# Attention memory and gated FFN on one core: heads grouped even and odd, 32-wide column tiles on both row halves, one load queue

## The chip, the core and the metric

The kernel runs on one core of a Trainium2 chip. A core has a matrix engine (TensorE, PE in the profile, with its weight loads as PEld), a vector engine (DVE), a scalar engine (ACT), GpSimd (POOL) and a sync engine (SP) that here only issues DMAs. They run side by side and wait for each other on semaphores. Products go to PSUM, from where ACT or DVE must copy them to the main on-chip memory. The metric is the time of one execution on the device, in microseconds.

## The reference

Per batch (8) and head (8), softmax weights over 32 memory slots, made from `phi`, gather k and v over 576 tokens into a memory of 32 rows. Queries attend to that memory, and the heads together (512 wide) go through a gated feed-forward block.

```python
a = phi - np.max(phi, axis=2, keepdims=True)
a = np.exp(a)
a = a / (np.sum(a, axis=2, keepdims=True) + 1e-09)   # axis 2: the tokens
k_m = np.einsum('bhsm,bhsd->bhmd', a, k)
v_m = np.einsum('bhsm,bhsd->bhmd', a, v)
scores = scale * np.matmul(q, k_m.transpose(0, 1, 3, 2))
...
attn = attn / (np.sum(attn, axis=-1, keepdims=True) + 1e-09)
x = np.matmul(attn, v_m)                 # then [4608, 512] over all heads
g = x @ w_gate                           # 512 -> 1536
silu = g * (1.0 / (1.0 + np.exp(-g)))
val = x @ w_val
return (silu * val @ w_out)              # 1536 -> 512
```

All tensors are float32; d is 64 per head.

## The kernel before

The order of the work is written by hand: each engine takes its instructions in the order in which the code issues them. `x` is never formed. Since `x @ w = attn @ (v_m @ w)`, the kernel multiplies the 32 memory rows of each head with its 64 rows of the weights, `U = v_m @ w`, and then the attention weights with `U`. Four heads make a group of 128 rows (4 x 32), and two groups make the 8 heads.

For one batch the steps are, with their lines:

- **Loads.** `phi` and `q` come through SP's queue in float32 (L71, L85), k and v through GpSimd's queue, converted to bfloat16 on the way (L79, L80). GpSimd then casts q (L93). GpSimd also issues the loads of the weights, six blocks `W` (L101) and three blocks `WO` (L110).
- **Memory.** `phi_exp` (L122) is one ACT instruction. `kv_group` (L134) multiplies pairs of heads, 64 memory rows wide, with k and v of both heads (256 columns); only the diagonal halves are wanted. L144 sums the weights with a column of ones, L152 inverts, L155 scales and masks on DVE. `kv_T` transposes (L165, copy L167).
- **Queries.** `q_T` transposes two heads at a time (L173, copy L179).
- **Attention.** `scores` multiplies 128 x 64 blocks of the masked memory with the queries (L188), ACT takes the exp (L196). `z_norm` sums over each head's 32 rows with a block matrix of ones (L203); ACT takes Ln and exp(-x) (L205, L207), DVE multiplies (L209).
- **U.** `u_step` makes one tile of 128 x 512 from two products, 64 wide, contracted over 128 rows (L218). ACT (L227, seven of twelve) or DVE (L229, five of twelve) copies it. There are twelve steps a batch: 3 column blocks, gate and value, 2 groups.
- **Slots.** `gv_slot`: 24 a batch (12 blocks of 128 hidden columns, two halves of 288 tokens). Four products (L248) write gate and value into one buffer of two PSUM banks; ACT takes silu of the gate (L256), DVE multiplies with the value (L262) into `t_h`. The multiplication is issued one slot later.
- **Output.** Twelve products of 512 columns per tile of 128 tokens (L286), a copy by DVE (L298) or ACT (L296), and DMAs on SP (L300). A pair of batches has nine tiles; four follow the even batch, five the odd one.

PSUM is shared by three pools of two buffers each: `gv` (two banks a buffer), `s` (memory, transposes, U) and `o` (output).

The main loop, for batch b: `window(b)` loads ACT's table for exp and Ln, issues the scores, the exp of phi(b+1), and the normalisation, with up to 36 output products of batch b-1 between them. Then `interleave` issues the 24 slots of batch b and spreads the rest of the output products and the preparation of batch b+1 (memory, queries, U) over them by the weights in ns that stand ahead of each item. Batch 0 differs: its U steps stand between its slots, and batch 1's preparation follows them. The output tiles of the last batch come after everything.

Of the kernel before, what the change touches and what calls it, by code (L numbers as in the profile page):

```python
# [14 lines left out]
def kernel(  # L15
# [10 lines left out]
):  # L26

# [11 lines left out]
    NG = 2  # L39
# [21 lines left out]
    ident = consts.tile([128, 128], BF16, tag="ident", name="ident")  # L61
    mask = consts.tile([128, 128], FP32, tag="mask", name="mask")
    bones = consts.tile([128, 128], BF16, tag="bones", name="bones")
    ones1 = consts.tile([128, 1], BF16, tag="ones1", name="ones1")


    phis, kvs, qs, qf = {}, {}, {}, {}

    def load_phi(b):
        t = inp.tile([P, H, J, M], FP32, tag="phi", name="t_phi")  # L70
        nc.sync.dma_start(  # L71
            out=t.rearrange("p h j m -> p h (j m)"),
            in_=phi[b].rearrange("h (p j) m -> p h (j m)", p=P),
        )
        phis[b] = t
# [7 lines left out]
    def load_q(b):  # L83
        t = inp.tile([P, H, J, D], FP32, tag="qf", bufs=1, name="t_qf")
        nc.sync.dma_start(  # L85
            out=t.rearrange("p h j d -> p h (j d)"),
            in_=q[b].rearrange("h (p j) d -> p h (j d)", p=P),
        )
        qf[b] = t

    def cast_q(b):
        t = inp.tile([P, J, H, D], BF16, tag="q", bufs=1, name="t_q")
        nc.gpsimd.tensor_copy(out=t.rearrange("p j h d -> p h j d"), in_=qf.pop(b))  # L93
        qs[b] = t
# [23 lines left out]
    ephis, bkvs, kvTs, qTs, atts = {}, {}, {}, {}, {}  # L118

    def phi_exp(b):  # L120
        t = att.tile([P, J, H, M], BF16, tag="ephi", name="t_ephi")
        nc.scalar.activation(  # L122
            out=t.rearrange("p j h m -> p h j m"), in_=phis.pop(b), func=AF.Exp
        )
        ephis[b] = t

    def kv_group(b, g):

        pk = ps.tile([128, 2 * 2 * D + 1], FP32, tag="s", name="p_kv")
        te, tk = ephis[b], kvs[b]  # L130
        for j in range(J):
            for pp in range(2):
                pr = 2 * g + pp
                nc.tensor.matmul(  # L134
                    pk[64 * pp:64 * pp + 64, 0:4 * D],
                    lhsT=te[:, j, 2 * pr:2 * pr + 2],
                    rhs=tk[:, :, 2 * pr:2 * pr + 2, j * D:(j + 1) * D],
                    start=(j == 0),
                    stop=(j == J - 1),
                )  # L140
        for j in range(J):
            for pp in range(2):
                pr = 2 * g + pp
                nc.tensor.matmul(  # L144
                    pk[64 * pp:64 * pp + 64, 4 * D:4 * D + 1],
                    lhsT=te[:, j, 2 * pr:2 * pr + 2],
# [4 lines left out]
        r = att.tile([128, 1], FP32, tag="rS", name="t_rS")  # L151
        nc.vector.reciprocal(out=r, in_=pk[:, 4 * D:4 * D + 1])  # L152
        t = att.tile([128, 2, 128], BF16, tag=f"bkv{g}", name="t_bkv")
        for w in range(2):
            nc.vector.scalar_tensor_tensor(  # L155
                out=t[:, w], in0=pk[:, 128 * w:128 * w + 128], scalar=r, in1=mask,
                op0=ALU.mult, op1=ALU.mult,
            )
        bkvs[b, g] = t

    def kv_T(b):
        pT = ps.tile([128, 2, NG, 128], BF16, tag="s", name="p_T")
        for g in range(NG):
            for w in range(2):
                nc.tensor.transpose(pT[:, w, g], bkvs[b, g][:, w], ident)  # L165
# [74 lines left out]
    def gv_slot(b, s):  # L240
# [20 lines left out]
        def mul():  # L261
            nc.vector.tensor_tensor(out=dst, in0=sg, in1=p[:, 1, 0:HALF], op=ALU.mult)  # L262
# [182 lines left out]
```

## Time and profile before

| | us |
|---|---|
| median of 3 runs (lowest, highest) | 334.71 (334.39, 336.28) |
| the profiled execution | 334.37 |
| its span | 332.5 |
| TensorE / ACT / DVE / GpSimd busy in the span | 272.5 / 177.5 / 165.1 / 41.8 |
| slot products L248, 768, mean 288 ns | 126.4 |
| output products L286, mean 379 ns | 102.8 |
| U products L218, 192, mean 403 ns | 34.3 |
| memory products L134 and L144, 192 each | 14.8 and 5.6 |
| GpSimd's casts of q, 8, mean 2745 ns | 22.0 |
| ACT table loads, 17 of 1283 ns | 21.9 |

Busy time is the union of an engine's instructions. Products are pipelined, so their mean durations overlap: a product of 512 columns has a mean of 379 ns, though 24 of them pass in 5.18 us. Idle time of an engine that nothing waits for costs nothing. The chain of waits follows the work back from the last instruction, at each step to what released it.

### The profile page before, as it was taken

To read this page: it belongs to the slowest core of one execution; us is meant where nothing else is said; L and a number is where in the kernel's file an instruction comes from. 1 tells how busy PE (TensorE), PEld (TensorE's weight loads), DVE (VectorE), ACT (ScalarE), POOL (GpSimd) and SP (SyncE) were. 2 spreads that over 40 slices of the span, in tenths; PEclk is the share of its full clock that TensorE was granted. 3 is DMA by queue.
4 is the path that set the end of the run, shared out by engine and by line. 5 is a ranking of instruction groups with operands and counts; after the bars stand their busy time and mean duration, and the time that the engine had idled before them with its cause. 6 is when DMAs were issued, how large, how long until landed. Compare 5 with 4: busy or idle time off the path is not lost.

```text
span 332.5 us, 5356 instructions
## 1 busy us (share of the span) xinstructions
PE 272.5 (82%) x2076; PEld 159.3 (48%) x2096; DVE 165.1 (50%) x371; ACT 177.5 (53%) x333; POOL 41.8 (13%) x39
## 2 busy tenths in 40 slices
PE   0044587878989899989998999989898999898894
PEld 0033144534565456645664467446644575445541
DVE  1012345563567354855576446745673558455520
ACT  4000855438446855496448744794378455764501
POOL 8025030050013000500050001300030000000000
PEclk9999999999999999999999999999999999999998
DMA  7999999891588055943891284917201210030033
GB/s 177 231 206 205 251 230 261 148 140 36 139 182 131 2 129 140 185 63 78 208 182 16 60 209 111 137 35 174 64 0 29 69 42 24 2 95 0 2 95 95
DMA packets 35624, 38.08 MB, mean 115 GB/s; under 512 B 1808, under 2 KB 30992, under 8 KB 35600
## 3 DMA queue, kind: packets, MB, share of 16 engines
q1 hardware_dynamic: 18304, 23.60, 28.5%
q0 software_dynamic: 17296, 14.16, 27.9%
q8 instruction: 16, 0.26, 0.3%
q14 instruction: 8, 0.07, 0.1%
HBM read 42.47 MB, written 9.44 MB: 156 GB/s over the span
## 4 chain that ended last, share of the span: by engine, by line
PE 64%; DVE 15%; DMA 7%; ACT 7%; issue 3%; POOL 2%; another core or an unknown queue 1%; SPq 0%; ACTq 0%; POOLq 0%
PE p_oo L286 24%; PE p_gv L248 24%; DVE t_h L262 8%; PE p_u L218 8%; DMA W<-in_moe_w_gate_dram 6%; ACT t_sg L256 4%; PE p_kv L134 3%; DVE t_qT L179 2%; DVE t_U L229 2%; DVE t_bkv L155 2%; PE p_q L173 2%; PE p_sc L188 1%; PE p_z L203 1%; ACT t_U L227 1%; POOL t_q L93 1%
## 5 line engine op out<-in xcount | busy, mean ns | idle before, releaser
L248 PE MATMUL p_gv<-t_A,t_U 128*128 128x288 bf16 x768 | 126.4, 288 | 14.1 <-DVE t_h L262 13.0
L256 ACT ACTIVATE t_sg<-p_gv 128x288 bf16<-128x288 f32 x192 | 79.0, 411 | 93.9 <-PE p_gv L248 60.9
L262 DVE TENSOR_TENSOR t_h<-t_sg,p_gv 128x288 bf16<-128x288 bf16 x192 | 86.2, 451 | 44.7 <-ACT t_sg L256 44.5
L286 PE MATMUL p_oo<-WO,t_h 128*128 128x512 bf16 x412 | 102.8, 379 | 1.3 <-issue 1.0
L248 PEld LDWEIGHTS <-t_U 128*128 128x128 bf16 x768 | 70.5, 98 | 60.5 <-issue 31.2
L286 PEld LDWEIGHTS <-t_h 128*128 128x128 bf16 x432 | 41.7, 98 | 38.5 <-issue 1.6
L218 PE MATMUL p_u<-W,t_kvT 128*64 128x512 bf16 x192 | 34.3, 403 | 6.2 <-ACT t_U L227 4.2
L227 ACT CAST t_U<-p_u 128x512 bf16<-128x512 f32 x56 | 32.1, 586 | 9.9 <-PE p_u L218 8.8
L229 DVE CAST t_U<-p_u 128x512 bf16<-128x512 f32 x40 | 27.7, 691 | 18.0 <-PE p_u L218 16.8
L298 DVE COPY t_o<-p_oo 128x512 f32<-128x512 f32 x24 | 16.5, 689 | 35.7 <-PE p_oo L286 35.7
L134 PE MATMUL p_kv<-t_kv,t_ephi 96*64 96x256 bf16 x192 | 14.8, 294 | 18.6 <-DMA t_kv<-in_v_dram 18.6
L93 POOL CAST t_q<-t_qf 96x3072 bf16<-96x3072 f32 x8 | 22.0, 2745 | 52.5 <-PE p_q L173 30.4
L79 POOL DMA_DIRECT2D t_kv<-in_k_dram x8 | 6.3, 792 | 141.1 <-PE p_kv L144 102.3
L218 PEld LDWEIGHTS <-t_kvT 128*64 128x64 bf16 x192 | 11.1, 108 | 24.9 <-issue 23.1
L196 ACT ACTIVATE t_E<-p_sc 128x576 bf16<-128x576 f32 x16 | 9.6, 648 | 24.5 <-PE p_sc L188 24.5
L173 PE MATMUL p_q<-ident,t_q 96*128 96x96 bf16 x192 | 14.1, 214 | 8.6 <-POOL t_q L93 7.8
L209 DVE TENSOR_TENSOR t_A<-t_E,t_rz 128x576 bf16<-128x576 bf16 x16 | 12.1, 758 | 17.2 <-ACT t_rz L207 17.2
L134 PEld LDWEIGHTS <-t_ephi 96*64 96x64 bf16 x192 | 10.2, 117 | 21.7 <-issue 21.7
L179 DVE COPY t_qT<-p_q 128x576 bf16<-128x576 bf16 x32 | 14.5, 455 | 10.8 <-PE p_q L173 10.7
L152 DVE RECIPROCAL t_rS<-p_kv 128x1 f32<-128x1 f32 x16 | 2.7, 169 | 30.4 <-PE p_kv L144 30.4
L173 PEld LDWEIGHTS <-t_q 96*128 96x128 bf16 x192 | 11.9, 102 | 10.2 <-POOL t_q L93 7.9
L122 ACT ACTIVATE t_ephi<-t_phi 96x1536 bf16<-96x1536 f32 x8 | 11.8, 1477 | 4.2 <-DMA t_phi<-in_phi_dram 4.2
(31 smaller groups left out, 116.3 us busy)
## 6 DMA issues: line engine op xcount, KB each, us to landing
t_qf<-in_q_dram SPq DMA_DIRECT2D x8, 1152.0 KB, 7.8
t_phi<-in_phi_dram SPq DMA_DIRECT2D x8, 576.0 KB, 5.4
t_kv<-in_k_dram POOLq DMA_DIRECT2D x8, 576.0 KB, 8.3
t_kv<-in_v_dram POOLq DMA_DIRECT2D x8, 576.0 KB, 10.4
out_dram<-t_o SPq DMA_DIRECT2D x24, 192.0 KB, 2.3
out_dram<-t_o SPq DMA_DIRECT2D x24, 128.0 KB, 2.4
W<-in_moe_w_gate_dram POOLq DMA_DIRECT2D x3, 512.0 KB, 21.4
W<-in_moe_w_val_dram POOLq DMA_DIRECT2D x3, 512.0 KB, 23.1
```

The source lines that it names most:

```text
L93: nc.gpsimd.tensor_copy(out=t.rearrange("p j h d -> p h j d"), in_=qf.pop(b))
L134: nc.tensor.matmul(pk[64 * pp:64 * pp + 64, 0:4 * D], lhsT=te[:, j, 2 * pr:2 * pr + 2], rhs=tk[:, :, 2 * pr:2 * pr + 2, j * D:(j + 1) * D] ...
L173: nc.tensor.transpose(pq[:, P * j:P * (j + 1)], qs[b][:, j, 2 * pr:2 * pr + 2], ident[0:P, 0:P],)
L179: nc.vector.tensor_copy(out=t, in_=pq)
L218: nc.tensor.matmul(p[64 * pp:64 * pp + 64, :], lhsT=kvTs[b][:, 1, g, 64 * pp:64 * pp + 64], rhs=W[which, c][:, 2 * g + pp], start=True, st ...
L227: nc.scalar.copy(out=t, in_=p)
L229: nc.vector.tensor_copy(out=t, in_=p)
L248: nc.tensor.matmul(p[:, which, 0:HALF], lhsT=Us[b, which, c, g][:, 128 * r:128 * (r + 1)], rhs=atts[b, g][:, hf], start=(g == 0), stop=(g ...
L256: nc.scalar.activation(out=sg, in_=p[:, 0, 0:HALF], func=AF.Silu)
L262: nc.vector.tensor_tensor(out=dst, in0=sg, in1=p[:, 1, 0:HALF], op=ALU.mult)
L286: nc.tensor.matmul(box["p"], lhsT=hts[c, jf][:, 128 * u:128 * (u + 1)], rhs=WO[jf], start=(jf == 0), stop=(jf == NJF - 1),)
L298: nc.vector.tensor_copy(out=t_o, in_=box["p"])
```

## The change

The heads are grouped even and odd instead of by fours in order: group g holds heads g, g+2, g+4, g+6. In the contraction of U the two heads of a pair (2i, 2i+1) lie in the two halves of the 128 rows, 64 each; in that of the scores the halves hold two halves of the tokens. With that, three kinds of products are issued on part of the array, by an explicit place (row, column):

```diff
-    def kv_group(b, g):
-        pk = ps.tile([128, 2 * 2 * D + 1], FP32, tag="s", name="p_kv")
...
+    def kv_half(b, g):
...
         for j in range(J):
+            for i in range(NP):
                 nc.tensor.matmul(
+                    pk[32 * i:32 * i + 32, 2 * D * g:2 * D * (g + 1)],
+                    lhsT=ephis[b][:, j, g, i],
+                    rhs=kvs[b][:, :, 2 * i + g, j * D:(j + 1) * D],
...
+                    tile_position=(0, 32 * i),
+                )
```

The memory takes 48 products of 128 columns instead of 24 of 256, and no masked halves. The sums take 12 instead of 24. The mask goes; DVE normalises with one reciprocal and two multiplications (`bk`, `bv`) instead of two reciprocals and four masked products. k is written twice, so that after the transposes (3 instead of 4) it lies in both row halves; v of the even heads lies in rows 0 to 63 and that of the odd heads in rows 64 to 127.

```diff
     def scores(b, g):
+        p = gv_banks()
+        for i in range(NP):
+            for r in range(2):
                 nc.tensor.matmul(
+                    p[r][32 * i:32 * i + 32, 0:HALF],
+                    lhsT=kTs[b][64 * r:64 * r + 64, g, 32 * i:32 * i + 32],
+                    rhs=qTs[b, i][64 * r:64 * r + 64, g],
...
+                    tile_position=(64 * r, 32 * i),
...
+    def u_round(b, which, c):
+        p = [ps.tile([128, CH], FP32, tag="s", name=f"p_u{g}") for g in range(NG)]
+        for i in range(NP):
+            for g in range(NG):
                 nc.tensor.matmul(
+                    p[g][32 * i:32 * i + 32, :],
+                    lhsT=kTs[b][64 * g:64 * g + 64, 2, 32 * i:32 * i + 32],
+                    rhs=W[which, c][64 * g:64 * g + 64, i],
...
+                    tile_position=(64 * g, 32 * i),
+                )
+        for g in range(NG):
...
+            if g == 0:
+                nc.scalar.copy(out=t, in_=p[g])
+            else:
+                nc.vector.tensor_copy(out=t, in_=p[g])
```

A round replaces two U steps: eight products of 32 rows and 512 columns, contracted over 64, in place of four of 64 rows, contracted over 128. The token halves are now the two row halves of the queries (tokens whose place in a run of six is even or odd), so `token_segments` sends the output rows to other places.

The buffer of gate and value is split in two pools, `g` and `v`, of two buffers of one bank each. They serve scores and sums too, so exp and Ln are issued by halves of 288 columns.

```diff
+    def gv_banks():
+        return [
+            ps.tile([128, CH], FP32, tag=("g", "v")[r], name=f"p_{'gv'[r]}") for r in range(2)
+        ]
...
-        p = ps.tile([128, 2, 512], FP32, tag="gv", name="p_gv")
+        p = gv_banks()
```

Loads: q is converted by its DMA in GpSimd's queue, without a cast. The queue holds k, v and q of batch 0, the weights, and then phi, k, v and q of batch 1, 2 and so on. SP loads only the first phi.

```diff
     def load_q(b):
+        t = inp.tile([P, H, J * D], BF16, tag="q", name="t_q")
+        nc.gpsimd.dma_start(out=t, in_=q[b].rearrange("h (p j) d -> p h (j d)", p=P))
...
+    load_phi(0, nc.sync)
+    load_kv(0)
+    load_q(0)
...
+    load_phi(1, nc.gpsimd)
+    load_kv(1)
     load_q(1)
```

Order: batch 0's output products follow its slots at once; batch 1's window has none beside it; the first twelve slots of batch 1 have nothing between them, and batch 2's preparation follows in the other twelve. In the later windows four output products go ahead of the table load. Some output products are held back for the next batch.

```diff
+    run(out_list(0))
+    run(att_items(1))
+    run(u_items(1))
+
+    backlog = []
+    hold = {1: 0, 2: 12, 3: 12, 4: 14, 5: 14, 6: 16, 7: 0}
...
+        if b == 1:
+            interleave(slots[:12], [])
+            flush_mul()
+            exp_tables()
+            phi_exp(2)
+            interleave(slots[12:], att_items(2) + u_items(2))
```

What that does to three queues:

GpSimd at the start, before, from the fifth of the six weight blocks on:

```order
L101 DMA W_117<-in_moe_w_gate_dram 128x4x512
L101 DMA W_119<-in_moe_w_val_dram 128x4x512
L79 DMA t_kv<-in_k_dram 96x8x384
L80 DMA t_kv<-in_v_dram 96x8x384
L110 DMA WO_124<-in_moe_w_out_dram 128x4x512
L110 DMA WO_126<-in_moe_w_out_dram 128x4x512
L110 DMA WO_128<-in_moe_w_out_dram 128x4x512
L93 CAST t_q<-t_qf 96x8x6x64
```

GpSimd at the start, after the change, from its first load on:

```order
L72 DMA t_kv<-in_k_dram 96x8x384
L73 DMA t_kv<-in_v_dram 96x8x384
L78 DMA t_q<-in_q_dram 96x8x384
masks.py:197 MEMSET ident 128x128
masks.py:199 ISA
masks.py:199 AFFINE_SELECT ident<-ident 128x128
L86 DMA W_101<-in_moe_w_gate_dram 128x4x512
L86 DMA W_103<-in_moe_w_val_dram 128x4x512
```

q of batch 0 stood behind all weight loads and two loads of batch 1, as a cast; it is now the third load, ahead of the weights.

ACT in batch 1's window and slots, before (`t_E` exp of the scores, `t_ephi` of phi, `t_sg` silu of a slot):

```order
L348 ACT_TABLE_LOAD
L196 ACTIVATE t_E<-p_sc 128x576 x2
L122 ACTIVATE t_ephi<-t_phi 96x8x6x32
L205 ACTIVATE t_lz<-p_z 128x576
L207 ACTIVATE t_rz<-t_lz 128x576
L205 ACTIVATE t_lz<-p_z 128x576
L207 ACTIVATE t_rz<-t_lz 128x576
L256 ACT_TABLE_LOAD
L256 ACTIVATE t_sg<-p_gv 128x288 x8
L296 COPY t_o<-p_oo 128x512
L256 ACTIVATE t_sg<-p_gv 128x288 x9
```

ACT from the middle of batch 1's window on, after the change:

```order
L220 ACTIVATE t_lz<-p_v 128x288
L221 ACTIVATE t_lz<-t_lz 128x576
L273 ACT_TABLE_LOAD
L273 ACTIVATE t_sg<-p_g 128x288 x12
L365 ACT_TABLE_LOAD
L114 ACTIVATE t_ephi<-t_phi 96x4x6x32 x2
L273 ACT_TABLE_LOAD
L273 ACTIVATE t_sg<-p_g 128x288 x7
```

The exp of phi has moved out of the window into the middle of the slots, with a table load on either side.

DVE where a batch's U is made among the slots of the batch ahead of it, before:

```order
L229 CAST t_U<-p_u 128x512
L262 TENSOR_TENSOR t_h<-t_sg,p_gv 128x288
L229 CAST t_U<-p_u 128x512
L262 TENSOR_TENSOR t_h<-t_sg,p_gv 128x288 x2
L229 CAST t_U<-p_u 128x512
L262 TENSOR_TENSOR t_h<-t_sg,p_gv 128x288
```

DVE at a like place, after the change:

```order
L246 CAST t_U<-p_u_2263 128x512
L279 TENSOR_TENSOR t_h<-t_sg,p_v 128x288
L246 CAST t_U<-p_u_2286 128x512
L279 TENSOR_TENSOR t_h<-t_sg,p_v 128x288 x2
L246 CAST t_U<-p_u_2318 128x512
L279 TENSOR_TENSOR t_h<-t_sg,p_v 128x288
L246 CAST t_U<-p_u_2341 128x512
```

The pattern on DVE stays; each of its copies now belongs to a whole round (the other half of the round is ACT's), so a copy stands behind each round.

319 lines of the change are left out of this document (147 added, 172 removed).

## The prediction

> **What bounds the kernel now.** First the page's busy shares, and the shares of the chain that ended last:
>
> ```profile
> PE 272.5 (82%) x2076; PEld 159.3 (48%) x2096; DVE 165.1 (50%) x371; ACT 177.5 (53%) x333; POOL 41.8 (13%) x39
> PE 64%; DVE 15%; DMA 7%; ACT 7%; issue 3%; POOL 2%; another core or an unknown queue 1%; SPq 0%; ACTq 0%; POOLq 0%
> ```
>
> TensorE leads, but a third of the chain is something else. So I cut the span into five stages (view by stretches: the length, then busy time of PE, PEld, DVE, ACT, POOL, then the granted clock, DMA share and GB/s):
>
> ```profile
> 0.00:40.84 40.84, 10.83 (x97) 7.20 (x97) 6.78 (x25) 10.45 (x13) 14.90 (x22) 1.00 1.14 214
> 40.84:64.65 23.81, 18.91 (x114) 10.18 (x112) 12.67 (x27) 13.27 (x29) 2.74 (x1) 1.00 1.16 229
> 64.65:110.45 45.80, 40.56 (x359) 23.64 (x361) 26.79 (x61) 25.80 (x49) 8.55 (x6) 1.00 0.63 114
> 110.45:285.95 175.50, 164.65 (x1307) 97.99 (x1317) 101.34 (x226) 109.84 (x209) 15.57 (x10) 1.00 0.44 93
> 285.95:332.50 46.55, 37.52 (x211) 20.27 (x211) 17.50 (x34) 18.15 (x36) 0.00 (x0) 0.98 0.20 51
> ```
>
> A runs up to batch 0's first gate product, B over its 24 slots, C up to the window of batch 2, D over batches 2 to 6, E over batch 7 and the last output tiles. The granted clock is full (0.98 to 1.00), so only order and waits count. In A TensorE is busy 11 of 41 us; the chain in order of time and the timeline say why:
>
> ```profile
> 4.63 21.35 DMA W<-in_moe_w_gate_dram
> 26.26 0.74 POOL WO L110
> 27.00 2.76 POOL t_q L93
> 15.52 0.79 POOL L79 DMA_DIRECT2D t_kv<-in_k_dram  x1 [7.90 <-DMA t_kv<-in_k_dram]
> 18.63 1.49 PE L134 MATMUL p_kv<-t_kv,t_ephi 96*64 96x256 bf16 x12 [18.63 <-DMA t_kv<-in_v_dram]
> 29.81 1.14 PE L173 MATMUL p_q<-ident,t_q 96*128 96x96 bf16 x12 [7.82 <-POOL t_q L93]
> 40.84 3.88 PE L248 MATMUL p_gv<-t_A,t_U 128*128 128x288 bf16 x16
> ```
>
> k and v share the DMA engines with q and the second phi and land at 15.5 and 18.6. GpSimd's cast of q stands behind issues that wait for weights, so query transposes start at 29.8.
>
> In B, and in most of E, the slot loop is the bound:
>
> ```profile
> 52.55 0.90 ACT L256 ACTIVATE t_sg<-p_gv 128x288 bf16<-128x288 f32 x2 [0.74 <-PE p_gv L248]
> 52.99 0.94 DVE L262 TENSOR_TENSOR t_h<-t_sg,p_gv 128x288 bf16<-128x288 bf16 x2 [0.69 <-ACT t_sg L256]
> 53.50 1.14 PE L248 MATMUL p_gv<-t_A,t_U 128*128 128x288 bf16 x8 [0.50 <-DVE t_h L262]
> 55.13 0.66 PE p_gv L248 x4
> 190.40 0.49 PE p_gv L248 x4
> ```
>
> Two slots take 1.63 us (53.50 to 55.13), 0.82 each, while a slot's four products back to back take 0.49 (at 190.40). The product waits for DVE's multiplication, because one buffer holds both gate and value.
>
> **The change, stage by stage.**
>
> *A, the loads.* What the software queue does when it has the engines for itself:
>
> ```profile
> 66.65 0.77 POOL L79 DMA_DIRECT2D t_kv<-in_k_dram  x1 [21.59 <-PE p_kv L144]
> 67.41 0.77 POOL L80 DMA_DIRECT2D t_kv<-in_v_dram  x1
> t_kv<-in_k_dram POOLq DMA_DIRECT2D x1, 576.0 KB, 6.0
> t_kv<-in_v_dram POOLq DMA_DIRECT2D x1, 576.0 KB, 8.1
> 21.13 0.76 POOL L110 DMA_DIRECT2D WO<-in_moe_w_out_dram  x1 [1.58 <-DMA W<-in_moe_w_gate_dram]
> 23.67 0.74 POOL L110 DMA_DIRECT2D WO<-in_moe_w_out_dram  x1 [1.78 <-DMA W<-in_moe_w_val_dram]
> ```
>
> That k lands at 66.65 + 6.0 = 72.65 and v at 75.51: 2.86 us for 576 KB. Weight blocks land 2.54 apart (the two issues that wait for them). With bytes moving from about 3 us, phi, k, v and q are four times 2.86: v at some 11, q at some 14, and no cast behind it. From the cast's end (29.76) to the first gate product (40.84) took 11.1. Of that the exp of the next phi (1.48) leaves this window. Halved activations (four times 2 x 0.411 - 0.682 = 0.6, rows below) and the copies of the second round (0.1) come on top. First gate product: 14 + 11.1 - 1.5 + 0.7 = 24.3, **-16.5**. The weight blocks land from 16.5 to 29.2, the output blocks by 36.9, batch 1's inputs by 48.4: each ahead of its use below. Later batches' four loads (11.4) have a batch of over 30 us to hide in; behind GpSimd's waits stand only further loads.
>
> *B, the slots.* Gate and value now have two buffers each. A value buffer is busy from its slot's gate products on: 0.25 for them, 0.16 until the last result is out (0.65 - 0.49), ACT 0.44, DVE 0.49, 0.04 to TensorE: 1.38. Two slots and half a one must cover that, so a bare slot is 0.57, not 0.82. 24 slots take 13.7, twice two rounds of U (below) 4 x 1.31 = 5.2: 18.9 for 23.8, **-4.9**. Where output products fill the slots TensorE was nearly full, and little is won.
>
> *The narrow products.* What the trace shows of products side by side:
>
> ```profile
> 150.55 5.18 PE p_oo L286 x24
> 173.25 0.55 PE p_u L218 x4
> 173.81 0.60 PE p_gv L248 x4
> 162.98 0.78 PE p_kv L134 x12
> 163.48 0.35 PEld L144 LDWEIGHTS <-t_ephi 96*64 96x64 bf16 x12
> 178.15 0.69 DVE t_U L229
> ```
>
> 512 columns cost 0.216; four 64-wide p_u cost 0.55, not 0.86, so two column tiles do run together; the gate products behind them take 0.11 more than alone. A round now has eight 32-wide p_u for the same two tiles. Lower bound, all eight together: 0.25. Upper bound, one by one: 8 x 0.216 = 1.73. No row shows two row halves. I take 0.42, nearest to the row of weight loads: twelve, each with a one-column product, pass in 0.35, so eight pairs start within 7 x 0.029 = 0.20, and the last streams for 0.216. In the same way the memory products: 48 x 0.029 = 1.4 and 0.25 for the sums (bounds 0.9 and, at 0.78/12 each, 3.4), and scores 2 x 0.35 (bounds 0.3 and 16 x 0.122 = 1.95).
>
> Most of that gain meets the copies:
>
> ```profile
> L256 ACT ACTIVATE t_sg<-p_gv 128x288 bf16<-128x288 f32 x192 | 79.0, 411 | 93.9 <-PE p_gv L248 60.9
> L207 ACT ACTIVATE t_rz<-t_lz 128x576 f32<-128x576 f32 x16 | 10.9, 682 | 1.9 <-DVE t_A L209 1.6
> L348 ACT ACT_TABLE_LOAD x8 | 10.3, 1283 | 0.1
> L122 ACT ACTIVATE t_ephi<-t_phi 96x1536 bf16<-96x1536 f32 x8 | 11.8, 1477 | 4.2 <-DMA t_phi<-in_phi_dram 4.2
> L262 DVE TENSOR_TENSOR t_h<-t_sg,p_gv 128x288 bf16<-128x288 bf16 x192 | 86.2, 451 | 44.7 <-ACT t_sg L256 44.5
> L229 DVE CAST t_U<-p_u 128x512 bf16<-128x512 f32 x40 | 27.7, 691 | 18.0 <-PE p_u L218 16.8
> L179 DVE COPY t_qT<-p_q 128x576 bf16<-128x576 bf16 x32 | 14.5, 455 | 10.8 <-PE p_q L173 10.7
> L152 DVE RECIPROCAL t_rS<-p_kv 128x1 f32<-128x1 f32 x16 | 2.7, 169 | 30.4 <-PE p_kv L144 30.4
> ```
>
> A round fills both buffers of pool s, so the next one begins when DVE's copy is done: 0.69 + 0.04 + 0.42 + 0.16 = 1.31 per round, with a slot (0.6) inside it. DVE makes six copies a batch, five before (40 in 8). The new normalisation of k and v is 0.17 + 0.42 + 0.28 = 0.87 (widths 256 and 128, between the rows for 288 and 512 in slope 1.07 ns a column), about half of two reciprocals and four masked products.
>
> The Trainium skill, "TensorEngine Tiling (Array Packing)", PSUM Bottleneck, says that tiling speeds up TensorE but not the evacuation of PSUM. Here the 0.69 row agrees with it. Without that bound a round and its slot would cost 0.42 + 0.11 + 0.60 = 1.13, and the 35 or so rounds that stand one slot apart would take 6 us off the sum: 306; with it, 312.
>
> *C.* Batch 0's output products now stand alone: 48 x 0.216 + 0.6 = 11.0. Then batch 1: memory products 1.65, normalisation 0.87, transposes and their copy 0.7, the last two query copies 0.9: 4.2. Six rounds 7.9. A window with nothing to fill it: table load 1.28, four halved exps 1.65, twice Ln and exp 3.0, multiplication 0.76: 6.7. Twelve bare slots and the last multiplication 7.3. Two table loads and phi's exp in two parts, 4.2, in which ACT is shut to slots. Twelve slots with batch 2's preparation, bound by DVE: 12 x 0.451 + 0.87 + 4 x 0.455 + 0.35 + 6 x 0.691 = 12.6, with one wait 13. Sum 54.3 for 45.8, **+8.5**: output products that covered batch 1's window are spent before it.
>
> *D.* A batch's window: 36 output products 7.8, sums 0.5, scores 0.7, changes of form 0.2: 9.2; four of the products now go ahead of the table load. Slots with 12 output products: the 8 that carry them 6.5; 8 with memory and queries 9.0 (7.2 of TensorE; 1.0 while DVE normalises, 0.9 instead of 0.76 for a slot with a query copy); 7 with six rounds 7.6; one more 0.5: 32.8 a batch. With 22 output products 10.3 + 8.0 + 7.0 + 9.2 = 34.5. Three of the first and two of the second: 167.4 for 175.5, **-8.1**, of which 16 products (3.5) only move into E.
>
> *E.* Window 9.2, 24 slots with 28 products 24 x 0.49 + 28 x 0.216 + 0.3 = 18.1, and the tail as it was:
>
> ```profile
> 314.86 12.90 PE L286 MATMUL p_oo<-WO,t_h 128*128 128x512 bf16 x58
> ```
>
> From there to the end are 17.6: 44.9 for 46.55, **-1.7**. The 16 products fit where slots waited.
>
> Sum: 332.5 - 16.5 - 4.9 + 8.5 - 8.1 - 1.7 = 309.8 of span; the execution took 334.37, 1.9 more than its span: **312 us**. That execution is 0.1% under the median of 334.71. About 0.5% is what a measurement of this kernel can tell from no change.
>
> **Rivals.**
> 1. *All eight tiles stream together.* A round is 0.25, memory products 0.95, scores 0.3: 48 x 0.17 + 8 x 0.7 + 8 x 0.4 = 17, of which about two thirds reach the end, the rest lies under DVE: 301. For: the pairs in p_u. Against: no row shows more than two. The Trainium skill, "TensorE: Matmul & The Clock Gate", Measured speedup vs the span model, has packed tiles start some 4 ns apart; by it, an estimate, a round is 0.244. No run here shows that yet.
> 2. *Slower: row halves exclude each other.* The code alternates halves, so each product would wait for the one ahead: a round 1.73, +1.31 x 48 = 63; scores +1.25 x 8 = 10; some 10 hidden in waits for copies: 375. It decides from a round of 0.42 + 22/48 = 0.88 up. For: no row splits the array by rows. Against: it is shown to split by columns.
> 3. *Late loads.* Beside SP's four blocks k needed from 3 to 15.5; phi still runs beside it. If that delays k, v and q by 6 us, A gives back 6: 318. Against: one block stands there, not four.
> 4. *Slots stay at 0.82*, since DVE's other copies order them: B +6, C +3, D +5: 326. Against: the wait in the rows is for t_h, and the gate's buffer no longer hangs on it.
>
> **How the numbers follow.** The forecast (305 to 316) 0.52, rival 1 0.20, rival 3 0.10, rival 4 0.08, rival 2 0.08, no change 0.02. The range takes in rivals 1, 3 and 4 and leaves out the last two: 298 to 326. Faster 0.90, same 0.02, slower 0.08.
>
> **What would show it.** First query transpose near 14 us, first gate product near 24; bare slots 0.57 apart; a p_u round 0.4 long and, with one slot between, 1.3 apart behind t_U; batch 2's window near 98; batches of 33 and 34.5. It is wrong if a round takes over 0.9, if q comes after 18, or if bare slots still wait 0.5 for t_h.

## The result and the profile after

The changed kernel takes **311.02 us** (median; 309.05 to 311.54) against 334.55 (334.22 to 336.28) for the kernel before on the same chip: a ratio of **0.9281** (95% interval 0.9236 to 0.9327). Run once more, beside other kernels of this study, it took 310.16 (309.11 to 310.56): 0.9243 (0.9194 to 0.9292). Ratios compare fast runs only; one run reported below is slow, the profiled one of e2 (359.06). The forecast was 312, within 298 to 326.

The busy shares and the shares of the chain that ended last, from the page of the profiled execution (309.05 us, span 307.2):

```profile
PE 263.7 (86%) x2440; PEld 150.5 (49%) x2440; DVE 164.3 (53%) x354; ACT 175.9 (57%) x364; POOL 31.5 (10%) x46
PE 69%; ACT 13%; DVE 10%; DMA 4%; issue 2%; POOL 0%; DVEq 0%; ACTq 0%; POOLq 0%
```

The five stages A to E, cut at the same events as before (the length, then busy time of PE, PEld, DVE, ACT, POOL, then the granted clock, DMA share and GB/s):

```profile
0.00:23.51 23.51, 8.77 (x124) 4.96 (x124) 5.56 (x17) 8.51 (x15) 11.38 (x20) 1.00 1.13 192
23.51:43.86 20.35, 17.82 (x136) 10.50 (x130) 13.46 (x28) 13.57 (x30) 4.64 (x6) 1.00 1.24 214
43.86:98.22 54.36, 42.30 (x436) 23.48 (x434) 26.57 (x57) 29.96 (x56) 6.18 (x8) 0.81 0.91 162
98.22:261.04 162.82, 154.28 (x1516) 89.66 (x1517) 100.23 (x217) 105.18 (x224) 9.28 (x12) 1.00 0.40 79
261.04:307.20 46.16, 40.49 (x240) 21.88 (x240) 18.45 (x36) 18.66 (x40) 0.00 (x0) 0.98 0.25 64
```

| stage | before | forecast | measured |
|---|---|---|---|
| A, to the first gate product | 40.84 | 24.3 | 23.51 |
| B, batch 0's slots | 23.81 | 18.9 | 20.35 |
| C, to batch 2's window | 45.80 | 54.3 | 54.36 |
| D, batches 2 to 6 | 175.50 | 167.4 | 162.82 |
| E, batch 7 and the last tiles | 46.55 | 44.9 | 46.16 |

One number in these rows was not in the forecast at all: in C the granted clock is 0.81, where it had been 1.00 before.

The chain in order of time (start, length, what), at the places on which the terms rest:

```profile
2.93 10.79 DMA t_q<-in_q_dram
13.76 0.68 PE p_q L183 x6
...
54.22 0.78 PE p_kv L128 x48
...
62.62 0.83 PE p_u L233 x8
...
92.72 0.61 PE p_u L233 x8
93.33 0.58 ACT t_U L244
93.95 0.61 PE p_u L233 x8
```

q lands at 13.7 (forecast 14). The 48 memory products pass in 0.78. A round is 1.23 from start to start (92.72 to 93.95): 0.61 from its first product to the start of ACT's copy, and ACT's copy. At 62.62 the same products take 0.83 instead of 0.61: there the clock is half, as the last rows of this section show.

The slots, by ACT's row of time in batch 0 (a row with x3 groups three instructions) and by the groups of instructions (busy time, mean ns, idle time ahead of them and what ended it):

```profile
33.60 1.43 ACT L273 ACTIVATE t_sg<-p_g 128x288 bf16<-128x288 f32 x3 [0.46 <-PE p_g L265]
35.24 1.43 ACT L273 ACTIVATE t_sg<-p_g 128x288 bf16<-128x288 f32 x3 [0.20 <-PE p_g L265]
L265 PE MATMUL p_v<-t_A,t_U 128*128 128x288 bf16 x384 | 81.1, 294 | 7.7 <-DVE t_h L279 6.7 <-ACT t_U L244 0.7
L246 DVE CAST t_U<-p_u 128x512 bf16<-128x512 f32 x48 | 33.2, 691 | 17.2 <-PE p_u L233 17.2
```

Three bare slots take 1.64 (33.60 to 35.24), 0.55 each instead of 0.82. TensorE's idle time behind the multiplication is 6.7 where it was 13.0 in the kernel before:

```profile
L248 PE MATMUL p_gv<-t_A,t_U 128*128 128x288 bf16 x768 | 126.4, 288 | 14.1 <-DVE t_h L262 13.0
```

Whether tiles on both row halves run together, from TensorE's row of time in batch 2's window (scores; eight products listed one by one, the first three and the last two here):

```profile
99.12 0.29 PE L201 MATMUL p_g<-t_qT,t_kT 64*32 64x288 bf16 x1
99.12 0.29 PE L201 MATMUL p_v<-t_qT,t_kT 64*32 64x288 bf16 x1
99.13 0.29 PE L201 MATMUL p_g<-t_qT,t_kT 64*32 64x288 bf16 x1
...
99.14 0.29 PE L201 MATMUL p_g<-t_qT,t_kT 64*32 64x288 bf16 x1
99.14 0.29 PE L201 MATMUL p_v<-t_qT,t_kT 64*32 64x288 bf16 x1
```

Eight tiles start within 0.02 us and end together. The mechanism of rival 1 is real and that of rival 2 is not.

And the clock, in stretches of two and four us of the same execution:

```profile
24.00:28.00 4.00, 3.81 (x16) 2.17 (x16) 1.62 (x4) 2.99 (x6) 1.16 (x2) 1.00 1.24 206
60.00:62.00 2.00, 1.24 (x16) 0.21 (x8) 0.69 (x1) 0.61 (x2) 0.00 (x0) 0.50 1.23 276
74.00:76.00 2.00, 2.00 (x10) 1.26 (x9) 0.96 (x3) 0.82 (x2) 0.00 (x0) 0.50 0.00 0
88.00:90.00 2.00, 2.00 (x19) 1.65 (x18) 1.20 (x4) 0.43 (x2) 0.00 (x0) 0.50 1.15 190
```

From about 59.5 to 76.4 us and from 87 to 90 the clock is half. The first of these stretches begins behind 27 transposes (55.25 to 58) and the first round, and lasts through rounds and a window with nothing beside them. The second begins behind the stop for the exp of the third phi. The row at 24 us belongs to another matter: its clock is recorded as 1.00, but its 16 products take 3.81.

### The profile page after: what moved, and what is told of

Its sections match the earlier page's. It is cut to its first block, busy times and chain, and to the rows that moved or that the text cites. A ratio compares the mean times of both kernels' runs of the same rounds, so it can differ in the third digit from the quotient of the medians.

```text
span 307.2 us, 6178 instructions
## 1 busy us (share of the span) xinstructions
PE 263.7 (86%) x2440; PEld 150.5 (49%) x2440; DVE 164.3 (53%) x354; ACT 175.9 (57%) x364; POOL 31.5 (10%) x46
## 4 chain that ended last, share of the span: by engine, by line
PE 69%; ACT 13%; DVE 10%; DMA 4%; issue 2%; POOL 0%; DVEq 0%; ACTq 0%; POOLq 0%
PE p_oo L303 29%; PE p_v L265 14%; PE p_g L265 10%; PE p_u L233 9%; ACT t_U L244 6%; DMA t_q<-in_q_dram 4%; DVE t_h L279 3%; PE p_q L183 3%; DVE t_qT L189 2%; DVE t_U L246 2%; PE p_kv L128 2%; ACT t_lz L221 1%; ACT t_E L211 1%; ACT L365 1%; ACT t_lz L220 1%
## 5 line engine op out<-in xcount | busy, mean ns | idle before, releaser
L273 ACT ACTIVATE t_sg<-p_g 128x288 bf16<-128x288 f32 x192 | 78.2, 412 | 64.1 <-PE p_g L265 49.2
L279 DVE TENSOR_TENSOR t_h<-t_sg,p_v 128x288 bf16<-128x288 bf16 x192 | 84.4, 449 | 34.9 <-ACT t_sg L273 26.8
L265 PE MATMUL p_v<-t_A,t_U 128*128 128x288 bf16 x384 | 81.1, 294 | 7.7 <-DVE t_h L279 6.7
L265 PE MATMUL p_g<-t_A,t_U 128*128 128x288 bf16 x384 | 81.9, 295 | 3.5 <-DVE t_A L223 2.6
L233 PE MATMUL p_u<-W,t_kT 64*32 64x512 bf16 x384 | 27.1, 416 | 10.2 <-ACT t_U L244 7.0
L223 DVE TENSOR_TENSOR t_A<-t_E,t_lz 128x576 bf16<-128x576 bf16 x16 | 12.1, 758 | 32.1 <-ACT t_lz L221 32.1
L233 PEld LDWEIGHTS <-t_kT 64*32 64x32 bf16 x384 | 10.4, 90 | 25.4 <-issue 21.9
L128 PE MATMUL p_kv<-t_kv,t_ephi 96*32 96x128 bf16 x384 | 7.6, 231 | 12.4 <-DMA t_kv<-in_v_dram 11.0
L114 ACT ACTIVATE t_ephi<-t_phi 96x768 bf16<-96x768 f32 x16 | 12.6, 844 | 3.8 <-DMA t_phi<-in_phi_dram 3.7
L128 PEld LDWEIGHTS <-t_ephi 96*32 96x32 bf16 x384 | 6.0, 102 | 14.5 <-issue 12.5
```

The source lines that it names most:

```text
L128: nc.tensor.matmul(pk[32 * i:32 * i + 32, 2 * D * g:2 * D * (g + 1)], lhsT=ephis[b][:, j, g, i], rhs=kvs[b][:, :, 2 * i + g, j * D:(j + 1) ...
L233: nc.tensor.matmul(p[g][32 * i:32 * i + 32, :], lhsT=kTs[b][64 * g:64 * g + 64, 2, 32 * i:32 * i + 32], rhs=W[which, c][64 * g:64 * g + 64 ...
L265: nc.tensor.matmul(p[which][:, 0:HALF], lhsT=Us[b, which, c, g][:, 128 * o:128 * (o + 1)], rhs=atts[b, g][:, r], start=(g == 0), stop=(g = ...
L273: nc.scalar.activation(out=sg, in_=p[0][:, 0:HALF], func=AF.Silu)
L279: nc.vector.tensor_tensor(out=dst, in0=sg, in1=p[1][:, 0:HALF], op=ALU.mult)
```

## The experiments

All times are medians. "Slots of batch n" is the start of the multiplication that makes the second half of `t_A`, from DVE's row of time; slots follow it. These columns and the span are from the profiled run of each kernel.

| | median us (range) | ratio to before (95%) | slots of batch 0 | 1 | 2 | 7 | span |
|---|---|---|---|---|---|---|---|
| before | 334.55 | 1 | 38.85 | 83.27 | 117.93 | 293.40 | 332.5 |
| changed | 311.02 | 0.9281 | 21.54 | 72.23 | 105.59 | 267.93 | 307.2 |
| changed, again | 310.16 (309.11-310.56) | 0.9243 (0.9194-0.9292) | 23.61 | 73.59 | 106.71 | 269.03 | 308.3 |
| e1 loads alone | 329.10 (328.06-329.71) | 0.9809 (0.9736-0.9882) | 24.90 | 76.91 | 111.87 | 288.69 | 327.9 |
| e10 split alone | 318.67 (317.40-320.24) | 0.9501 (0.9442-0.9561) | 38.60 | 78.86 | 111.92 | 282.26 | 316.6 |
| e2 one buffer | 356.01 (353.65-359.06) | 1.0598 (1.0510-1.0686) | 24.49 | 81.17 | 119.75 | 315.41 | 357.3 |
| e2b one buffer | 329.79 (328.66-330.56) | 0.9810 (0.9734-0.9886) | 23.48 | 79.23 | 115.67 | 285.27 | 326.9 |
| e3 wide products | 316.99 (315.69-318.02) | 0.9456 (0.9390-0.9521) | 23.46 | 71.55 | 104.58 | 274.58 | 313.9 |
| e5 clock kept up | 308.56 (307.92-308.95) | 0.9204 (0.9147-0.9262) | 22.65 | 73.43 | 104.86 | 267.21 | 306.5 |
| e6 halves in turn | 307.79 (307.36-308.47) | 0.9160 (0.9091-0.9229) | 23.41 | 71.93 | 105.33 | 266.79 | 306.1 |
| e4 batch 1 regular | 304.08 (301.55-305.30) | 0.9038 (0.8956-0.9120) | 23.25 | 71.31 | 101.55 | 263.92 | 303.2 |
| e9 outputs as cover | 301.12 (300.65-303.09) | 0.8978 (0.8892-0.9064) | 23.06 | 66.99 | 97.33 | 259.70 | 299.0 |
| e11 e9 and e6 | 301.07 (298.57-302.59) | 0.8961 (0.8908-0.9014) | 23.11 | 65.82 | 96.14 | 257.45 | 296.8 |
| e12 warm start | 301.81 (300.80-302.75) | 0.8996 (0.8951-0.9041) | 23.17 | 68.92 | 100.36 | 261.66 | 301.0 |

### Loads alone (e1)

The kernel before with the loads of the change alone: one queue in order of need, q converted by its DMA with two buffers, the exp of the second phi behind batch 0's slots with a table load of its own, and each query transpose in two of 64 columns.

```diff
-    load_phi(0)
+    load_phi(0, nc.sync)
+    load_kv(0)
     load_q(0)
-    load_phi(1)
...
-    cast_q(0)
+    load_phi(1, nc.gpsimd)
+    load_kv(1)
     load_q(1)
...
+            flush_mul()
+            nc.scalar.preload_act_table_set("natural_log_exp_and_others")
+            phi_exp(1)
...
```

> [...] By the term for A: first gate product near 24 to 25 instead of 40.8, batch 0's 24 slots still 23 to 24 long, a table load and an exp (2.8) added behind them of which 1.5 leaves the first window: 334.6 - 16.5 + 1.3 = about 319 (316 to 322). Rival (the gain is given back because batch 1's inputs come after they are wanted): the copies of batch 1's inputs end near 48, so a wait of several us stands in front of batch 1's memory products and the time is 324 or more.

329.10: the rival's number, but not by the rival's wait. The first gate product comes at 27.27 (24 to 25 was expected). Batch 0's slots begin 14.0 earlier (24.90 for 38.85), but batch 1's only 6.4 (76.91 for 83.27). Two stretches between them:

```profile
50.00:55.00 5.00, 1.64 (x14) 0.98 (x15) 1.36 (x3) 3.70 (x5) 0.16 (x1) 0.97 1.30 204
55.00:60.00 5.00, 4.62 (x74) 3.81 (x71) 2.38 (x8) 0.00 (x0) 2.15 (x3) 0.50 1.24 229
60.00:65.00 5.00, 4.62 (x37) 1.84 (x37) 2.72 (x5) 1.60 (x3) 0.78 (x1) 0.50 1.22 197
```

From 50 to 55 TensorE works 1.64 us, while ACT loads its table and takes the exp of the second phi: work that stood beside other work before. TensorE's pause of 3.29 ahead of batch 1's memory products ends with that exp, not with a load. Behind it the clock is 0.50, and it stays so to 70. So the loads gain 14 of the 16.5 that were forecast, and more than half of that is lost again at once. The transposes in halves cost this kernel a little more in every batch (slots of batch 2 to 7: 176.8 for 175.5).

### One buffer for gate and value (e2, e2b), and two buffers alone (e10)

```diff
-        return [
-            ps.tile([128, CH], FP32, tag=("g", "v")[r], name=f"p_{'gv'[r]}") for r in range(2)
-        ]
+        p = ps.tile([128, 2, CH], FP32, tag="gv", name="p_gv")
+        return [p[:, 0], p[:, 1]]
```

> The changed kernel, with gate and value again in one tile of two banks (two buffers). By the term for B: bare slots go from 0.55 back to 0.82 us, 24 of them in batch 0 (+6), 12 in batch 1 (+3), and the slots between rounds and memory products of batches 2 to 7 lose some 1 us a batch (+5): 311 + 14 = 325 (320 to 330). Rival (the slots are ordered by DVE's other work or by ACT at 0.41 us each, and the buffers hardly matter): 311 to 315, with bare slots under 0.65.

356.01, far above both. The window shows why (TensorE's row of time, in batch 2):

```profile
118.16 0.40 PE L218 MATMUL p_gv<-t_E,bones 128*128 128x288 bf16 x1 [1.39 <-ACT t_lz L219]
118.35 6.21 PE L302 MATMUL p_oo<-WO,t_h 128*128 128x512 bf16 x22
124.40 0.65 PE L264 MATMUL p_gv<-t_A,t_U 128*128 128x288 bf16 x4
```

The second half's sum now waits for the logarithm of the first, as they share a tile, and 22 output products queue behind it. This comes with the edit and is not what the buffer costs in the slots. e2b issues both sums ahead of both logarithms:

> As e2 (gate and value in one tile of two banks), with both sum products of a group ahead of both logarithms. In e2 the second sum product had to wait for the first logarithm, since both halves were one tile: TensorE stood 1.15 and 1.39 us in each window with the output products queued behind, and the first gate product came 4.65 us after the second t_A began (119.75 to 124.40) where the changed kernel has 1.48 (105.59 to 107.07): some 3.2 us in each of seven windows, 22 in all, and 0.8 for the longer chain. Theory: without that the one buffer itself costs what the term for it says, 0.27 in bare slots: 356 - 22 - 6 = about 326 (320 to 331). Rival (one buffer costs 0.27 in nearly all 192 slots, also those with output products): 340 or more.

329.79: undoing the split costs 19 us (329.79 - 311.02), 5 more than the 14 that rival 4 had. By the table 5 of it lie between the slots of batch 0 and 1, 3 between those of 1 and 2, 7 from there to batch 7 and 2 behind; 2 more are inputs that landed later in this execution. The other way round, the split alone in the kernel before:

> The kernel before with gate and value (and the two halves of scores and sums) in two buffers of their own each, and the activations that read them halved; nothing else. By the terms as forecast (B -5, C -3, D -5) less some 2 for the halved activations: 334.9 - 11 = 324 (320 to 328). Second theory (as large as undoing it in the changed kernel, 329.8 - 311.0 = 18.8): 316. Rival (in the kernel before the preparation and output products are spread over all slots and fill the waits already, so only batch 0's slots gain): 330.

318.67, **15.9 less than before** (334.55), between the two theories and nearer to the second: 4.2 from the slots of batch 0 to those of batch 1 (40.26 for 44.42), 6.7 from there to the slots of batch 7 (203.40 for 210.13, about 1.1 a batch), and 4.8 behind these (34.34 for 39.10). The last had no price in my terms: in batch 7 no preparation and only 12 output products stand between 24 slots, so they gain 0.2 each.

### The products wide again (e3)

```diff
-        for i in range(NP):
-            for g in range(NG):
+        for g in range(NG):
+            for pp in range(2):
                 nc.tensor.matmul(
-                    p[g][32 * i:32 * i + 32, :],
-                    lhsT=kTs[b][64 * g:64 * g + 64, 2, 32 * i:32 * i + 32],
-                    rhs=W[which, c][64 * g:64 * g + 64, i],
+                    p[g][64 * pp:64 * pp + 64, :],
+                    lhsT=kvTs[b][:, 1, g, 64 * pp:64 * pp + 64],
+                    rhs=W[which, c][:, 2 * g + pp],
```

> The changed kernel with the products of the kernel before (block-diagonal keys and values by a mask, 64-wide tiles over all 128 rows, neighbouring heads in a group; query transposes of 64 columns), in the changed schedule, loads and gate/value buffers. By my account the copies of a round pace it, so the narrow products bring little: 48 rounds at 0.05 to 0.15, 8 times 1.2 for memory products and 0.7 for their normalisation, half of these hidden: 311 + 10 = 321 (315 to 326). Rival (the narrow products are what the change lives on, since all eight run together): 328 or more. Second rival (they are wholly hidden): 311 to 313.

316.99: 6 to 7 us above the changed kernel. TensorE's row of time in the same part of batch 2, for the wide products:

```profile
113.99 0.84 PE L127 MATMUL p_kv<-t_kv,t_ephi 96*64 96x256 bf16 x12
114.67 0.33 PE L137 MATMUL p_kv<-ones,t_ephi 96*64 96x1 bf16 x12
114.86 0.82 PE L127 MATMUL p_kv<-t_kv,t_ephi 96*64 96x256 bf16 x12
115.51 0.33 PE L137 MATMUL p_kv<-ones,t_ephi 96*64 96x1 bf16 x12
115.77 0.42 PE L247 MATMUL p_g<-t_A,t_U 128*128 128x288 bf16 x2
...
126.50 0.67 PE L216 MATMUL p_u<-W,t_kvT 128*64 128x512 bf16 x4
127.69 0.66 PE L216 MATMUL p_u<-W,t_kvT 128*64 128x512 bf16 x4
```

Memory takes 1.78 (113.99 to 115.77) against 1.10 (0.78 and 0.32 for the sums) in the changed kernel: 0.68 a batch, 5.4 in all. Its query transposes, which are 64 wide here, take 0.38 for 0.25, some 4 in all, and are no part of the change. Of both a share lies beside other work, so the narrow products bring between 2 (all of the 4 on the path) and 7 us. This is a net figure: by the table e3 loses 7.7 between the slots of batches 2 and 7 (170.00 for 162.34), but gains 1.9 to 2.6 between those of batch 0 and 1 (48.09 for 49.98 and 50.69). There its wide products last longer, and its clock is 1.00 up to 68 us, through the rounds in which the changed kernel has 0.50. The rounds of the later batches give nothing: with wide products they are 1.19 apart (126.50 to 127.69), no longer than the 1.23 of the changed kernel. The wide code issues one group after the other, the changed one alternates; the next experiment is about that.

### Row halves in turn (e6)

```diff
-        for i in range(NP):
-            for g in range(NG):
+        for g in range(NG):
+            for i in range(NP):
```

> The changed kernel with the loops over tiles turned round: in scores and rounds all four products of the upper 64 rows, then all four of the lower. Theory (eight tiles are independent of each other, and start some 0.01 to 0.03 apart in any order): no change, 310 to 312. Rival (row halves run together only when they alternate): four and four, a round 0.2 longer, 48 x 0.2 = +10 and more: 318 to 322.

Both theories missed: 307.79, some 2.4 us *faster* than the changed kernel (307.36 to 308.47, against 309.05 to 311.54 in all runs of the other; the kernel before had the same times beside both). Two rounds one slot apart in batch 2:

```profile
125.56 0.56 PE L233 MATMUL p_u<-W,t_kT 64*32 64x512 bf16 x8
126.65 0.66 PE L233 MATMUL p_u<-W,t_kT 64*32 64x512 bf16 x8
```

1.09 from round to round, for 1.23. A round and the copies around it, first in the changed kernel, then in e6:

```profile
121.90 0.59 ACT L244 CAST t_U<-p_u 128x512 bf16<-128x512 f32 x1 [0.31 <-PE p_u L233]
121.94 0.69 DVE L246 CAST t_U<-p_u 128x512 bf16<-128x512 f32 x1 [0.18 <-PE p_u L233]
122.54 0.55 PE L233 MATMUL p_u<-W,t_kT 64*32 64x512 bf16 x8
123.14 0.59 ACT L244 CAST t_U<-p_u 128x512 bf16<-128x512 f32 x1 [0.34 <-PE p_u L233]
```

```profile
121.79 0.59 ACT L244 CAST t_U<-p_u 128x512 bf16<-128x512 f32 x1 [0.25 <-PE p_u L233]
122.43 0.56 PE L233 MATMUL p_u<-W,t_kT 64*32 64x512 bf16 x8
122.87 0.59 ACT L244 CAST t_U<-p_u 128x512 bf16<-128x512 f32 x1 [0.18 <-PE p_u L233]
```

Each row half writes a PSUM tile of its own. ACT empties the first in 0.59, DVE the second in 0.69. Either way a round starts 0.05 after ACT's copy ends. Where products alternate, the second product of the round waits for DVE, whose copy ends at 122.63, and behind it, in TensorE's order, six more, of which three could have run: ACT's next copy comes 0.60 after the round's start. In turn, the upper half's four run as soon as ACT is done, and ACT's next copy comes after 0.44. By the table 1.5 of the gain lies between the slots of batch 0 and 1 (48.52 for 49.98 in the repeated run) and 0.9 between those of batches 2 and 7 (161.46 for 162.32), so most of what later rounds gain is hidden.

### The clock (e5)

```diff
+    def warm(n):
+        p = ps.tile([128, DM], FP32, tag="o", name="p_warm")
+        for _ in range(n):
+            nc.tensor.matmul(p, lhsT=ident, rhs=W[0, 0][:, 0], start=True, stop=True)
...
```

> The changed kernel with 54 added products of 512 columns whose result nobody reads, put where TensorE stands still in batch 1: 2 behind each of four preparation steps and each of six rounds, 12 and 14 in the window, 16 during the stop for the exp of the third phi. Theory: between 59 and 76 us and at 87 to 90 the granted clock is 0.50 because TensorE was too little in use just before, and this costs about 5 us; with TensorE kept in use the clock stays at 1.00, rounds of batch 1 fall from 1.46 to about 1.25, its first slots from 0.96 to 0.55, and the time is 306 to 309 in spite of more work. Rival (the half clock has another cause, such as the total work before, and idling does not matter): the clock is 0.50 in the same place and the added products, now 0.43 each, make it slower: 313 to 320.

(The list in that text adds up to 62 products, which is what ran.) 308.56: faster than the changed kernel by 1.6 to 2.5 us with more work. Rounds and window of batch 1:

```profile
60.00:66.00 6.00, 5.39 (x51) 1.90 (x50) 3.26 (x6) 2.63 (x5) 0.78 (x1) 1.00 1.22 245
66.00:73.40 7.40, 7.25 (x55) 3.28 (x55) 1.88 (x3) 6.16 (x13) 0.00 (x0) 1.00 0.92 143
```

The clock is 1.00 where it had been 0.50. Up to the slots of batch 1 the added products take as much as the clock gives (50.78 from the slots of batch 0, for 49.98 and 50.69); from there to those of batch 2 it is 31.43 for 33.12 and 33.36. What is left over is a lower bound for the price, since the added products stand in the queue too (3% of this kernel's chain).

### Batch 1 in the order of the later batches (e4, e9), and both gains together (e11)

```diff
-    run(out_list(0))
+    o0 = out_list(0)
+    run(o0[:14])
     run(att_items(1))
-    run(u_items(1))
+    for n, x in enumerate(u_items(1)):
+        x[1]()
+        run(o0[14 + 3 * n:17 + 3 * n])
-    backlog = []
+    backlog = o0[32:]
...
-        if b == 1:
-            interleave(slots[:12], [])
-            flush_mul()
-            exp_tables()
-            phi_exp(2)
-            interleave(slots[12:], att_items(2) + u_items(2))
...
```

This is e9; e4 has 24 output products ahead, none between rounds, 24 in the window.

> The changed kernel with batch 1 in the order of the later batches: 24 of batch 0's 48 output products ahead of batch 1's preparation, the other 24 in batch 1's window, where the exp of the third phi stands too, and batch 2's preparation spread over all 24 slots. Theory (the +8.5 of the term for C comes from this order, and the half clock from windows and rounds with nothing in them): the stop of 4.6 us and 5.2 us of output products leave the path, the clock stays at 1.00 in the window: 311 - 6 = 305 (302 to 308). Rival (batch 2's inputs come too late for this, or DVE's work in batch 1's slots sets the pace anyway): 309 to 312.

> As e4, with the 48 output products of batch 0 laid where TensorE would wait: 14 ahead of batch 1's preparation (until its inputs are there), 3 behind each of the six rounds, 16 in the window. Theory: each round has 0.65 of products beside its copies, so TensorE is never slack for long and the clock stays at 1.00: first round to window no longer than in e4 though 18 products are done in it: 302 (299 to 305). Rival (the three products behind each round stand in front of the next one and lengthen it by as much): as e4 or 1 to 2 us more.

304.08 and 301.12: both times came as expected, but one sign of e4 did not. Its clock did not stay at 1.00 but is 0.50 from 55 to 68 us, through its rounds and most of its window. In e9 the rounds of batch 1, with real work between them, keep the clock:

```profile
54.00:58.00 4.00, 4.00 (x42) 1.36 (x41) 2.36 (x5) 1.83 (x4) 0.00 (x0) 1.00 1.32 206
58.00:62.00 4.00, 4.00 (x45) 1.47 (x44) 2.54 (x4) 2.88 (x5) 0.00 (x0) 1.00 1.19 240
```

TensorE is busy all the time, 18 output products pass beside the six rounds, and the slots of batch 2 start 8.3 earlier than in the changed kernel (97.33 for 105.59).

> e9 and e6 together: batch 1 in the order of the later batches with output products as cover, and the row halves in turn. e6 was 3 us faster than the changed kernel, since the first four products of a round write only the buffer that ScalarE empties first and need not wait for VectorE's: rounds one slot apart took 1.09 (121.34, 122.43; 124.48, 125.56, 126.65) for 1.24. If both gains add: 301.1 - 3 = 298 (296 to 300). Rival (e6's gain lay in the rounds of batch 1 that e9 covers with output products): 300.5 to 301.5.

301.07 by the median, though its profiled run was 298.57: by the medians no gain over e9, as the rival said. Its six runs fall in two: 298.57 and 298.79 with a mean granted clock of 0.992 to 0.993, and 300.84 to 302.59 with 0.980 to 0.981. Those of e9 do so too: 300.65 to 301.45 with 0.990 to 0.991, and 303.09 with 0.979. At like clock e11 is some 2 us faster, so the gains do seem to add, and the medians hide it because e11 had the lower clock in four runs of six and e9 in one of four. Why one kernel's clock differs from run to run is not shown. Both e9 and e11 are faster than the kernel before and the changed one.

### Products ahead of the first inputs (e12) and the changed kernel again

> e11 with some 170 added products of 128 columns before batch 0's first gate product, of which nobody reads the result: 80 while the first inputs are on their way, the rest in the gaps of batch 0's preparation and window. Theory (until about 28 us products run at half rate because TensorE was hardly used, although the granted clock is recorded as 1.00): memory products fall from 1.47 to 0.85, the first ten gate and value products from 0.48 apart to 0.25, and the time by 2 to 3 us against e11: 295.5 (294 to 297). Rival (the half rate lies in something else than idling, for instance the DMA traffic at that time): the products stay at half rate, the added ones delay the work, and it is 1 to 4 us slower than e11.

301.81: no faster, though the theory's own sign came. TensorE's row of time and stretches of time:

```profile
13.13 0.85 PE L128 MATMUL p_kv<-t_kv,t_ephi 96*32 96x128 bf16 x48 [1.77 <-DMA t_kv<-in_v_dram]
48.13 0.85 PE L128 MATMUL p_kv<-t_kv,t_ephi 96*32 96x128 bf16 x48 [1.94 <-DMA t_kv<-in_v_dram]
24.91:43.01 18.10, 15.77 (x133) 9.52 (x130) 13.30 (x28) 12.71 (x29) 4.64 (x6) 1.00 1.24 212
50.00:54.00 4.00, 3.21 (x31) 2.43 (x32) 2.42 (x7) 0.00 (x0) 0.83 (x2) 0.54 1.22 236
```

Memory products of batch 0 take 0.85 for 1.47, and batch 0's slots 18.10 where the changed kernel had 20.35. In e11, which lacks only the added products, these slots take 19.5 (25.06 to 44.58). So the products of the first 28 us did run at half rate for want of use. But what is won ends in a wait: batch 1's v lands at 48, TensorE waits 1.94 for it, and then the clock is 0.54. There the loads now set batch 1's start.

> The changed kernel once more, beside e11 and e12, to see whether e6's 307.8 differs from it and not the chip from another hour: 310 to 311.5 if the order of row halves is the cause; 307.5 to 308.5 if it is not.

310.16, as expected if the order of row halves is what makes e6 faster.

## Why the prediction was right, step by step

**The sum was right with errors that cancel.** 309.8 of span was forecast, 307.2 measured: D came 4.6 lower, A 0.8 lower; B and E came 1.5 and 1.3 higher. That 312 lies so near to 311.02 is in part luck. Tried one by one, the split of the buffers is worth 16 to 19 (e10, e2b), the loads 5.7 (e1, beside 334.81) and the narrow products 2 to 7 (e3), while the order of batch 1 costs 6 to 9 (e4, e9). Holding output products back and the halved activations were not tested alone.

**A.** First gate product 23.51 for 24.3. In the repeated run of the same kernel v and q landed 2 us later (first memory product 13.03, not 10.97), and its slots begin 2.1 later: rival 3 in small, from one execution to the next. In the profiled runs of all other kernels with these loads the slots begin later than here (22.65 to 24.90, not 21.54), so some of A's gain on the forecast is luck.

**B.** The slot was right (0.55 for 0.57) and the sum 1.5 short, because half rate was not thought of. A row that the prediction quotes had shown it: 16 slot products in 3.88 at 40.84, twice the time of four in 0.49; the clock column said 1.00 and I took it at its word. With the row halves in turn and batch 1 in the later order e11 has 19.5, and with the rate mended as well e12 has 18.1, for the forecast 18.9.

**The split of gate and value** is the largest part of the change: 15.9 alone, 19 when undone (13 to 14 by the terms). "Where output products fill the slots TensorE was nearly full, and little is won" failed for batch 7.

**The narrow products.** Their duration was mis-sized upwards: memory with its sums 1.10, not 1.65; DVE's normalisation keeps TensorE waiting 0.52, not 1.0. Both stand between the last output product in batch 2's slots and its first round. These nine slots ("8 with memory and queries" and "one more") took 7.81 (113.58 to 121.39) and not 9.5. That is more than the batch's whole error, 31.23 (98.22 to 129.45) for 32.8: the window was 0.35 shorter than forecast, the eight slots with output products were right (6.51 for 6.5), and the seven with rounds took 0.5 more. A round that waits for nothing lasts 0.41 from its first start to its last end (124.61), so without the 0.16 of the last result it is 0.25, rival 1's figure, and not 0.42. The interval between rounds came out nearly right all the same, 1.23 to 1.24 for 1.31; by the sum with 0.25 it would be 1.14, and the 0.09 over that is not accounted for. That the copies pace the rounds was argued as "most of that gain meets the copies", and the rows of e6's section bear it out; e6 shows that the order of issue, not only the copies' length, keeps the gain away. Rival 1 had its tiles but not its time: the kernel was not bound by that. The Trainium skill, "TensorE: Matmul & The Clock Gate", Measured speedup vs the span model, has tiles start some 4 ns apart. The 0.02 for eight scores agree.

**C.** 54.36 for 54.3, out of pieces that were off both ways, which is luck. Rounds took 8.70 for 7.9 and bare slots 8.0 for 7.3, both where the clock was half, and the stop 4.6 for 4.2; output products 10.4 for 11.0, the window 6.25 for 6.7, the last slots 12.4 for 13. That the order of batch 1 costs 8.5 is near the mark: e4 takes 6.1 off the changed kernel (310.16 to 304.08), with the clock still half in its rounds, and e9 9.0 (to 301.12), with the clock kept.

**E.** 1.3 over: the window was 10.0 (261.04 to 271.06) for 9.2; slots 18.2 for 18.1. That it gains little on the kernel before is not for want of a faster slot (e10: 4.8 off): the held output products take it.

**The clock.** "The granted clock is full, so only order and waits count" held for the kernel before and not for the changed one, which made TensorE's work shorter and left its waits in one place (e3, with wide products in the same order, keeps a mean clock of 0.980 to 0.984, the changed kernel has 0.953 to 0.967). For the price there is e5's lower bound of 1.6, and the kernel before against itself: its runs with a mean clock of 0.997 to 0.999 took 334.0 to 335.0, with 0.988 335.9 and 336.0, with 0.969 338.6 to 339.0. That is 4.1 us for 9.8 us of lost clock (0.029 x 337). The changed kernel loses 11 (0.037 x 307): at the same rate 4.7, an estimate.

## What to carry to other kernels

When a change makes the matrix engine's work shorter, look at what its new gaps do to its clock, and lay work that must be done anyway (here output products) into them rather than issuing it in one block. Where two engines empty two buffers, issue all products for one buffer ahead of those for the other, as an in-order queue hands the slower engine's pace on to the faster one. Price a second buffer in every stage where a wait for it can stand, the last one too.

## What the runs showed of the hardware

- Eight products on tiles of 64 rows and 32 columns start within 0.02 us and last 0.29 at 288 columns, as one does (the slots' products of 288 columns have a mean of 0.294).
- The clock fell to half at about 59.5 us though no pause of TensorE ahead of it was over 0.7 us; there were 27 transposes and short products in the four us ahead. It came back after 3.2 us of dense slots (73.2 to 76.4). The Trainium skill, "TensorE: Matmul & The Clock Gate", What's actually happening, has the clock fall after an idle window of about 3.4 us and return after as long a busy one. The return agrees with this trace, while the fall came without an idle stretch. In e1 it fell behind a pause of 3.29 us.
- The same transposes do not always end so. In e4 (51.9 to 54.6) the clock is 0.83 from 54 to 55 us and 0.50 behind it. In e9 (49.7 to 52.4) it stays at 1.00, with dense output products from 53.4 on. What decides between them stays open.
- In the first 28 us the record of the granted clock says 1.00 while products of 288 columns stand 0.24 apart instead of 0.12. The Trainium skill, "TensorE: Matmul & The Clock Gate", Seeing it yourself, warns that these records are unreliable. Here they miss the first stretch and show the later ones.
